# The fold of the input moved into the transform's first products, and the second stage's split and transpose issued two slots ahead

## The chip, the core and the metric

The kernel runs on one core of a Trainium2 chip. The core's engines work side by side, each through a queue of its own in program order: TensorE (PE in the profile, with its weight loads shown as PEld), VectorE (DVE, in the text also V), ScalarE (ACT), GpSimd (POOL) and SyncE (SP), which here issues most of the transfers. The metric is the time in device microseconds (us) that one execution takes.

## The reference

The reference takes eight batches of 3072 x 256 numbers through three steps:

```
X = fft(fft(x, axis=1), axis=2).real                    # 8 x 3072 x 256
x = X.reshape(24576, 256)
h = x @ w_in                                            # 256 -> 2048
x = (max(h, 0) + log1p(exp(-|h|))) @ w_out              # softplus, 2048 -> 256
e = argmax(normalized x . normalized expert_emb / tau)  # one of 8 experts for each token
out = gate * (max(x @ w1[e], 0) @ w2[e])                # 256 -> 1024 -> 256
```

All of it is wanted in 32-bit precision.

## The kernel before

**Numbers in two halves.** TensorE multiplies 16-bit floats, so each operand is split into a high half and a low half, `hi = fp16(v)` and `lo = fp16(v - hi)`, and a product is three matmuls (hi·hi, hi·lo, lo·hi) summed in PSUM.

**First stage: transform, first layer, routing.** It goes through 256 units, each a batch b (8), one of 8 tiles `ti` of 384 tokens and one quarter `i` of the 2048 hidden values. A unit's 64 matmuls are `pu` and `pv` (even and odd part of the first product) and `G` (the product with `w_out`, three units late). ScalarE and VectorE make the softplus of it: `h` (L806, L813, L814), `e` (L822 to L836), and then `gh` and `gl`, the two halves of the scaled result. Per unit either GpSimd makes `gh` in one instruction of 1536 columns (L847) and VectorE makes `gl` for all 1536 (L860), or GpSimd also takes the last 384 columns of both (L847 with 1152, L849, L850, L851) and VectorE's `gl` has 1152. Which of them is decided while the program is written, by a budget for GpSimd in each unit: `room[0]` begins at `ROOM` = 3.6, less 2.6 for each low half of the input that waits for GpSimd and 3.4 for each fold that GpSimd gets, less 1.4 per scatter of routed rows; the longer form of a unit wants 1.2, a step in the preparation of the second stage's weights (`wprep`, L1338 to L1343) wants 2.1 and is held back while `busy[0]` is set.

Beside its 32 units a batch has the next batch's transform done, in two phases. In the first (`fft_a`, `ph[0] == "a"`) a loop over eight pieces `xt` of the input, 96 x 1024 numbers, makes the products `psa` (12 matmuls of 96 columns for each half of a piece, two halves), whose result is evicted into `U_s` by ScalarE (L677) and VectorE (L678). Before a piece can be multiplied it passes three steps, spread over units by the lists `ORDER` and `BORD`: `split_fold` ("sp") replaces its two column halves by their sum and difference (`x_fold`, L490 to L495; for pieces 0, 2, 3, 6 and 7 on VectorE, else on GpSimd), `split_hi` ("sa") scales it (L617) and rounds it to 16 bits (L618) on ScalarE, and `split_lo` ("sq") takes the low half on GpSimd (L610). In the second phase the products `psb`, `psc` and `psd` follow. Batch 0 is transformed ahead of the units, and there the fold is already left to the products: with `boot[0] and PEF`, each `psa` half is 24 matmuls over both column halves of the input, and a negated copy `fan` of the table `fa_s` gives the difference.

**Second stage: the experts.** The routed rows lie sorted by expert in a bucket in DRAM and are taken in 104 slots of up to 256 rows (`phase2`). Slot j: load of the rows of slot j+3 (`p2_load`, SP), `p2_m1(j, 0)` (24 matmuls into `psH`, evicted by ScalarE's `hh` L1209 and VectorE's `hl` L1210), `p2_split(j+1)` (L1179, L1180: two pairs on VectorE that make `xs`), `p2_tr(j+1)` (L1187: SP's DMA transpose of `xs` to `xT`, which `p2_m1(j+1)` multiplies), `p2_m1(j, 1)`, then for slot j+2 the norm (`p2_norm`, L1144 to L1170, on ScalarE, GpSimd and VectorE) with the copy of its expert's weights on VectorE in its middle (L1135), and `p2_m2(j)` (48 matmuls into `psO`, evicted by ScalarE's `ot` L1233, then scattered by GpSimd L1235). `xs` has one buffer, `xT` two, the rows four. `ahead()` is called three times in a slot; from slot 6 to 16 each call issues one of 32 loads of the experts' weights `W` (512 KB each). The generator `phase2` is advanced step by step, three times in each of the last units and once in each turn of the loop that ends the routing.

Instructions are issued on every engine in the order in which the program is written (`tc.manual_schedule`). The line 206 in the profile is the helper that issues every matmul.

Of the kernel before, what the change touches and what calls it, by code (L numbers as in the profile page):

```python
# [11 lines left out]
F16 = mybir.dt.float16  # L12
# [26 lines left out]
ROOM = 3.6  # L39
# [103 lines left out]
def fft_moe_moe(ctx, tc, x, w_in, w128, w_out, emb, tau, w1, w2, fa, db, mcs, tid, ident, tri, misc, out,  # L143
# [27 lines left out]
    fa_s = bigf.tile([96, 2, 96], F16, name="fa_s")  # L171
    xp = pF.enter_context(tc.tile_pool(name="xp", bufs=2, side="right"))
# [178 lines left out]
    fan = bootp.tile([96, 2, 96], F16, name="fan")  # L351
# [250 lines left out]
    def on_v(b, k):  # L602
        return k in (FW1 if b == 1 else FW)

    sp2, sp3 = [], []

    def split_lo():
        for b, k, xt, xh in sp3:
            xl = xp.tile([96, 4, 256], F16, tag="xl", name="xl", bufs=3)
            G.tensor_tensor(xl, xt, xh, op=ALU.subtract)  # L610
            xs[b, k] = (xh, xl)
        sp3.clear()

    def split_hi():
        for b, k, xt in sp2:
            xh = xp.tile([96, 4, 256], F16, tag="xh", name="xh", bufs=3)
            A.activation(xt, xt, AF.Copy, scale=scal[b]["sx"][0:96])  # L617
            A.activation(xh, xt, AF.Copy)  # L618
            sp3.append((b, k, xt, xh))
        sp2.clear()  # L620

    def split_fold():


        for b, k in late:
            xt = xs.pop((b, k))
            x_fold(xt, V if on_v(b, k) else G)
            sp2.append((b, k, xt))
        late.clear()
# [14 lines left out]
    def fft_a(b):  # L644
# [4 lines left out]
        for k in range(8):  # L649
            if k + 2 < 8:  # L650
                x_get(b, k + 2)
            while late and late[0] == (b, k) or sp2 and sp2[0][:2] == (b, k) or sp3 and sp3[0][:2] == (b, k):
                split_lo()
                split_hi()
                split_fold()
            xh, xl = xs.pop((b, k))
            for c in range(2):
                ps = fps("psa")
                for j in range(4):
                    o = ps[:, j * 96:(j + 1) * 96]  # L660
                    cs = slice(c * 128, (c + 1) * 128)
                    if boot[0] and PEF:
# [576 lines left out]
    def phase2():  # L1239
# [5 lines left out]
        p2_split(0)  # L1245
        yield
        p2_tr(0)
        yield
# [6 lines left out]
        for j in range(nslot):  # L1255
# [19 lines left out]
            if j + 1 < nslot:  # L1275
                p2_split(j + 1)
                p2_tr(j + 1)
# [3 lines left out]
            if j + 2 < nslot:  # L1281
# [4 lines left out]
                p2_wcopy(j + 2)  # L1286
                for _ in nrm:
                    pass
# [72 lines left out]
    with tc.manual_schedule():  # L1361
# [89 lines left out]
        for s in range(len(units) + LAG + 1):  # L1451

            room[0] = ROOM - 2.6 * len(sp3) - 3.4 * sum(not on_v(*t) for t in late)
            nsc = min(len(scq), 2 if cur[0] // 8 >= npair - SNAP or len(scq) > 5 else 1) if room[0] > 0 else 0
            room[0] -= 1.4 * nsc
            busy[0] = bool(sp3) or room[0] < 2.1
# [83 lines left out]
            def tail():  # L1540
                if "row1" in p2 and (u is None or not S2[0].get("xs")):
# [8 lines left out]
                       x2=lambda: x2(2), r1=route, r2=route, r3=route, sp=split_fold, sa=split_hi, sq=split_lo, wp=wp.step, sc=lambda: scatters(nsc), p1=tail, p2=tail, p3=tail,  # L1550
# [54 lines left out]
```

## Time and profile before

| what | value |
|---|---|
| median of three runs | 3485.12 us (3482.34 to 3485.62) |
| profiled execution | 3496.98 us |
| its span, first to last instruction | 3495.2 us |
| PE, DVE, ACT, POOL busy | 88%, 80%, 65%, 61% of the span |
| mean granted TensorE clock | 0.957 of full speed |
| softplus sums of the units (L836), first to last start | 122 to 2334 us |
| first-layer matmuls of the experts, first to last start | 2333.4 to 3483.7 us |

The two stages meet at about 2333 us. Busy shares are means over stages with different limits, so a stage is read by its own rows. A wait that the profile lists belongs to the engine that stood, and names the instruction whose end ended it. Rows are given with the line of the kernel, the engine, the operation and the tiles, written as result<-inputs.

### The profile page before, as it was taken

Reading aid. Unit: us, or ns where it says so; the run is one execution under the profiler, and the core shown is the slowest. Engines: PE = TensorE matmul, PEld = TensorE weight load, DVE = VectorE, ACT = ScalarE, POOL = GpSimd, SP = SyncE. Lnnn points to the kernel's source line nnn. Section 1 sums busy time; section 2 is a strip of 40 time slices with the busy share of each in tenths; the row PEclk is TensorE's granted clock in tenths of the full one; section 3 lists DMA queues with packets and bytes.
Section 4 is the critical chain, followed back from the end, with each engine's and each line's share of the span. In section 5 each row is a group of like instructions: output and inputs, shape, how many; then the busy total and the mean of one; then the engine's idle time right before and its main releaser. Section 6 shows DMA issues by size and latency. Waiting matters only on the chain.

```text
span 3495.2 us, 76414 instructions
## 1 busy us (share of the span) xinstructions
PE 3078.9 (88%) x31264; PEld 2740.8 (78%) x31264; DVE 2796.1 (80%) x4488; ACT 2260.5 (65%) x3400; POOL 2138.7 (61%) x1855
## 2 busy tenths in 40 slices
PE   3788898888987988888988999998889999999997
PEld 3677787876876877777887899877778888888886
DVE  7779898988888989988988988984557777777776
ACT  5777777767877878867877888763344444444443
POOL 5357677776786777777777787662234444444443
PEclk8899998998999999999999999999899999999999
DMA  4111210311211211211111000114643333332221
GB/s 138 48 49 53 71 57 28 101 40 38 73 52 51 80 42 62 80 46 51 50 46 31 19 17 20 65 38 107 175 117 76 75 75 80 75 75 74 73 73 38
DMA packets 197088, 223.74 MB, mean 64 GB/s; under 512 B 119028, under 2 KB 154751, under 8 KB 196480
## 3 DMA queue, kind: packets, MB, share of 16 engines
q1 hardware_dynamic: 177920, 167.32, 18.1%
q0 software_dynamic: 18816, 51.54, 4.2%
q8 instruction: 244, 4.00, 0.5%
q14 instruction: 108, 0.88, 0.1%
HBM read 122.91 MB, written 70.71 MB: 55 GB/s over the span
## 4 chain that ended last, share of the span: by engine, by line
issue 29%; PE 24%; DVE 20%; POOL 12%; ACT 10%; DMA 4%; POOLq 0%; SPq 0%; DVEq 0%; ACTq 0%
PE G L206 12%; DVE e L836 5%; PE pu L206 4%; POOL out_dram L1235 3%; DVE gl L860 3%; PE pv L206 3%; ACT e L831 2%; POOL gh L847 2%; ACT e L827 2%; DVE h L814 2%; DVE h L813 2%; PE psb L206 2%; PE psH L206 1%; ACT e L822 1%; POOL xt L495 1%
## 5 line engine op out<-in xcount | busy, mean ns | idle before, releaser
L847 POOL TENSOR_SCALAR gh<-e,sc 128x1536 f16<-128x1536 f32 (+1 forms) x256 | 620.8, 2425 | 493.5 <-DVE e L836 333.2
L206 PE MATMUL G<-wo_s,gh 128*128 128x264 f16 x6144 | 832.7, 284 | 2.2 <-POOL gh L850 2.0
L206 PEld LDWEIGHTS <-gh 128*128 128x128 f16 x6144 | 602.7, 101 | 100.2 <-POOL gh L850 3.3
L206 PE MATMUL psH<-xT,wb 128*128 128x256 f16 (+1 forms) x4992 | 560.3, 274 | 67.1 <-DMA xT<-xs 66.5
L836 DVE SCALAR_TENSOR_TENSOR e<-h,e 128x1536 f32<-128x1536 f32 x256 | 531.6, 2077 | 75.3 <-ACT e L831 71.8
L206 PEld LDWEIGHTS <-wb 128*128 128x128 f16 x4992 | 480.2, 100 | 137.7 <-DMA xT<-xs 78.3
L206 PEld LDWEIGHTS <-win_s 128*128 128x128 f16 x6144 | 534.0, 100 | 24.6 <-DVE h L814 11.6
L206 PE MATMUL psO<-wb,hh 128*128 128x256 f16 x3200 | 529.8, 273 | 0.6 <-ACT hh L1209 0.6
L206 PE MATMUL G<-wo_s,gl 128*128 128x264 f16 x3072 | 440.3, 281 | 28.6 <-DVE gl L860 28.4
L1147 POOL TENSOR_TENSOR nr<-ssq,half 128x2 f32<-128x2 f32 (+1 forms) x104 | 237.5, 2284 | 355.3 <-ACT jk L1144 355.0
L860 DVE SCALAR_TENSOR_TENSOR gl<-e,sc,gh 128x1536 f16<-128x1536 f32 (+1 forms) x256 | 451.0, 1762 | 3.6 <-POOL gh L847 2.2
L206 PE MATMUL psO<-wb,hl 128*128 128x256 f16 x1600 | 436.2, 273 | 0.6 <-DVE hl L1210 0.5
L1209 ACT ACTIVATE hh<-psH 128x512 f16<-128x512 f32 (+1 forms) x416 | 239.6, 579 | 269.7 <-PE psH L206 263.8
L1210 DVE SCALAR_TENSOR_TENSOR hl<-psH,hh 128x512 f16<-128x512 f32 (+1 forms) x416 | 268.7, 666 | 181.4 <-ACT hh L1209 173.3
L822 ACT ACTIVATE e<-h 128x1536 f32<-128x1536 f32 x256 | 378.0, 1477 | 47.7 <-DVE h L814 46.7
L1235 POOL DMA_INDIRECT out_dram<-ot,r x200 | 202.3, 1011 | 311.2 <-ACT ot L1233 272.3
L831 ACT ACTIVATE e<-e 128x1536 f32<-128x1536 f32 x256 | 379.5, 1482 | 4.0
L827 ACT ACTIVATE e<-e 128x1536 f32<-128x1536 f32 x256 | 378.4, 1478 | 0.0
L206 PE MATMUL pu<-pqh,win_s 128*128 128x192 f16 (+1 forms) x2048 | 371.6, 251 | 3.8 <-ACT h L806 3.8
L206 PEld LDWEIGHTS <-gl 128*128 128x128 f16 x3072 | 303.3, 100 | 89.0 <-DVE gl L860 38.5
L206 PEld LDWEIGHTS <-hh 128*128 128x128 f16 x3200 | 312.6, 98 | 36.8 <-ACT hh L1209 0.7
L813 DVE SCALAR_TENSOR_TENSOR h<-pv,sc,h 128x768 f32<-128x768 f32 (+1 forms) x256 | 258.7, 1011 | 99.2 <-ACT h L806 50.5
(274 smaller groups left out, 5902.8 us busy)
## 6 DMA issues: line engine op xcount, KB each, us to landing
xt<-in_x_dram SPq DMA_DIRECT2D x114, 384.0 KB
r<-bucket SPq DMA_DIRECT2D x96, 268.0 KB
wt<-in_w_dram SPq DMA_DIRECT2D x16, 1024.0 KB
wsc<-wo SPq DMA_DIRECT2D x32, 512.0 KB
W<-wsc SPq DMA_DIRECT2D x32, 512.0 KB
raw<-in_w_in_dram SPq DMA_DIRECT2D x8, 512.0 KB
raw<-in_w_out_dram SPq DMA_DIRECT2D x8, 512.0 KB
wb<-wsc SPq DMA_DIRECT2D x2, 2048.0 KB
```

The source lines that it names most:

```text
L206: T.matmul(o, l, r, start=start, stop=stop)
L813: V.scalar_tensor_tensor(h[:, :, n:384], pv[:, :, s0:n], sc["ninv"], h[:, :, s0:n], op0=ALU.mult, op1=ALU.add)
L822: A.activation(e, h, AF.Abs)
L827: A.activation(e, e, AF.Exp, scale=-1.0)
L831: A.activation(e, e, AF.Ln, bias=1.0)
L836: V.scalar_tensor_tensor(flat(d["e"]), flat(d["h"]), 0.0, flat(d["e"]), op0=ALU.max, op1=ALU.add)
L847: G.tensor_scalar(gh[:, 0:n], e[:, 0:n], sg, 1.0, op0=ALU.mult, op1=ALU.mult)
L860: V.scalar_tensor_tensor(flat(d["gl"]), flat(d["e"]), scal[u[0]]["sg"], flat(d["gh"]), op0=ALU.mult, op1=ALU.subtract)
L1147: G.tensor_tensor(nr[:, 0:nt], ssq[:, 0:nt], half[:, 0:nt], op=ALU.pow)
L1209: A.activation(h2, p_, AF.Relu)
L1210: V.scalar_tensor_tensor(l2, p_, 0.0, h2, op0=ALU.max, op1=ALU.subtract)
L1235: no_dep(G.indirect_dma_start(out=out, out_offset=bass.IndirectOffsetOnAxis(ap=rows.bitcast(I32)[:, t, 264:265], axis=0), in_=ot, in_offse ...
```

## The change

In the first stage the fold instructions are gone for batches 1 to 7 too: `psa` is always made of 24 matmuls, with `fan` kept for the whole stage. A piece passes two steps, both straight from the loaded input: ScalarE scales and rounds in one instruction, and the low half is one VectorE instruction (scale and subtract). The "sp" step does nothing. `ROOM` is 4.8 and takes no account of the splits any more, and `busy[0]` is no longer set in the loop.

In the second stage slots 0 and 1 are split and transposed before the loop, and inside slot j it is slot j+2 that is split and transposed: after its weights are copied and the first part of its norm is made, and before `p2_m2(j)`.

```diff
-ROOM = 3.6
+ROOM = 4.8
...
+    fan = bigf.tile([96, 2, 96], F16, name="fan")
...
-    fan = bootp.tile([96, 2, 96], F16, name="fan")
...
+    def split_hi():
+        for b, k in late:
+            xt = xs.pop((b, k))
+            xh = xp.tile([96, 4, 256], F16, tag="xh", name="xh", bufs=3)
+            A.activation(xh, xt, AF.Copy, scale=scal[b]["sx"][0:96])
+            sp3.append((b, k, xt, xh))
+        late.clear()
     def split_lo():
         for b, k, xt, xh in sp3:
             xl = xp.tile([96, 4, 256], F16, tag="xl", name="xl", bufs=3)
-            G.tensor_tensor(xl, xt, xh, op=ALU.subtract)
+            V.scalar_tensor_tensor(xl, xt, scal[b]["sx"][0:96], xh, op0=ALU.mult, op1=ALU.subtract)
...
-    def split_hi():
-        for b, k, xt in sp2:
-            xh = xp.tile([96, 4, 256], F16, tag="xh", name="xh", bufs=3)
-            A.activation(xt, xt, AF.Copy, scale=scal[b]["sx"][0:96])
-            A.activation(xh, xt, AF.Copy)
...
-    def split_fold():
-        for b, k in late:
-            xt = xs.pop((b, k))
-            x_fold(xt, V if on_v(b, k) else G)
...
-                    if boot[0] and PEF:
+                    if PEF:
...
-        p2_split(0)
-        yield
-        p2_tr(0)
-        yield
+        for j in range(min(2, nslot)):
+            p2_split(j)
+            yield
+            p2_tr(j)
+            yield
...
             p2_m1(j, 0)
             yield
             ahead()
-            if j + 1 < nslot:
-                p2_split(j + 1)
-                p2_tr(j + 1)
             p2_m1(j, 1)
...
                 p2_wcopy(j + 2)
+                next(nrm)
+                p2_split(j + 2)
+                p2_tr(j + 2)
                 for _ in nrm:
                     pass
             p2_m2(j)
...
-            room[0] = ROOM - 2.6 * len(sp3) - 3.4 * sum(not on_v(*t) for t in late)
+            room[0] = ROOM
             nsc = min(len(scq), 2 if cur[0] // 8 >= npair - SNAP or len(scq) > 5 else 1) if room[0] > 0 else 0
             room[0] -= 1.4 * nsc
-            busy[0] = bool(sp3) or room[0] < 2.1
```

How the instructions of the engines stand in the program, before and after, at three places.

GpSimd in the first stage, a stretch of batch 3's transform, before (`gh<-e,sc` of 1536 columns is the short form of a unit, `xt<-xt` a fold, `xl` a low half, `bucket` a scatter):

```order
L847 TENSOR_SCALAR gh<-e,sc 128x1536
L490 TENSOR_TENSOR xt<-xt 96x4x128
L494 TENSOR_SCALAR xt<-xt 96x4x128
L495 TENSOR_TENSOR xt<-xt 96x4x128
L847 TENSOR_SCALAR gh<-e,sc 128x1536
L959 MEMSET gap 1x8
L960 DMA bucket<-rows,dst 198912x268
L959 MEMSET gap 1x8
L960 DMA bucket<-rows,dst 198912x268
L610 TENSOR_TENSOR xl<-xt,xh 96x1024
```

The same engine in the same part of the program, after:

```order
L835 TENSOR_SCALAR gh<-e,sc 128x1152
L837 TENSOR_SCALAR e<-e,sc 128x384
L838 TENSOR_SCALAR gh<-e 128x384
L839 TENSOR_TENSOR gl<-e,gh 128x384
L947 MEMSET gap 1x8
L948 DMA bucket<-rows,dst 198912x268
```

Folds and low halves are gone from GpSimd, and the units have the long form: 255 of them in the whole program, before 115. On VectorE 36 folds of two instructions go, 56 instructions `xl<-xt,sc,xh` come, and `gl` has 1152 columns in 255 units.

VectorE in a slot of the second stage, from the evictions of `p2_m1(j, 0)` on, before (`wb<-W` is the weights' copy, `u`, `s`, `nr`, `dn` and `gm` belong to the norm of slot j+2):

```order
L1179 TENSOR_SCALAR xs<-r,s_35404 128x256
L1180 SCALAR_TENSOR_TENSOR xs<-r,s_35404,xs 128x256
L1179 TENSOR_SCALAR xs<-r,s_35404 128x256
L1180 SCALAR_TENSOR_TENSOR xs<-r,s_35404,xs 128x256
L1210 SCALAR_TENSOR_TENSOR hl_35531<-psH,hh_35530 128x512 x2
L1133 TENSOR_LOAD ti__27853
L1133 ISA x2
L1135 ISA
L1135 COPY wb_27850<-W 128x4097
L1150 TENSOR_SCALAR u<-nr 128x2
```

A slot after, from the copy on:

```order
L1123 COPY wb_29387<-W 128x4097
L1138 TENSOR_SCALAR u<-nr 128x2
L1139 TENSOR_SCALAR u<-u 128x2
L1141 TENSOR_SCALAR s_37157<-u 128x2
L1143 TENSOR_SCALAR s_37157<-u 128x2
L1167 TENSOR_SCALAR xs<-r,s_37157 128x256
L1168 SCALAR_TENSOR_TENSOR xs<-r,s_37157,xs 128x256
L1167 TENSOR_SCALAR xs<-r,s_37157 128x256
L1168 SCALAR_TENSOR_TENSOR xs<-r,s_37157,xs 128x256
L1145 TENSOR_SCALAR nr<-nr 128x2
L1146 RECIPROCAL nr<-nr 128x2
L1148 SCALAR_TENSOR_TENSOR u<-r,nr 128x2
```

The four instructions of the split have moved from between the evictions of the slot to behind the weights' copy, ahead of the rest of the norm (`u<-r,nr` is what ScalarE's L1164 waits for).

SP in a slot in which `W` is loaded, before (`r` is the load of rows, `zt` a clearing of rows):

```order
L1113 DMA bucket<-zt 128x268
L1116 DMA W<-wsc 128x2048 x2
L1187 DMA_TRANSPOSE xT<-xs 128x8x128
L1116 DMA W<-wsc 128x2048
L1126 ISA
L1126 DMA r<-bucket 128x2x268
```

And after:

```order
L1101 DMA bucket<-zt 128x268
L1104 DMA W<-wsc 128x2048 x3
L1175 DMA_TRANSPOSE xT<-xs 128x8x128
L1114 ISA
L1114 DMA r<-bucket 128x2x268
```

The transpose stands behind all three weight loads of its slot, and it is that of slot j+2 instead of j+1. The first `W` loads stand in slot 5, before in slot 6.

## Rows read from the trace of the kernel before

**Rows 1.** Busy us by stretch: length, PE, PEld, DVE, ACT, POOL, clock, DMA, GB/s.

```profile
412.00:1988.00 1576.00, 1368.18 (x14743) 1217.75 (x14742) 1389.92 (x1637) 1211.20 (x1337) 1178.84 (x900) 0.95 0.17 52
2104.00:2206.00 102.00, 102.00 (x1037) 93.61 (x1035) 91.42 (x96) 86.72 (x77) 75.87 (x71) 1.00 0.05 18
2600.00:3400.00 800.00, 782.78 (x7130) 695.23 (x7128) 583.26 (x1412) 355.95 (x1039) 357.42 (x370) 1.00 0.31 75
```

**Rows 2.** Lines between 412 and 1988 us: count, duration ns min/median/max.

```profile
L836 DVE SCALAR_TENSOR_TENSOR e<-h,e x178: 1736/1759/4910, 415.2 to 1987.5; 128x1536 f32<-128x1536 f32 x178
...
L860 DVE SCALAR_TENSOR_TENSOR gl<-e,sc,gh x177: 1396/1805/4339, 417.0 to 1982.9; 128x1536 f16<-128x1536 f32 x112, 128x1152 f16<-128x1152 f32 x65
...
L492 DVE SCALAR_TENSOR_TENSOR xt<-xt x29: 686/1487/2495, 499.9 to 1949.4; 96x512 f32<-96x512 f32 x29
...
L847 POOL TENSOR_SCALAR gh<-e,sc x177: 1217/2642/3615, 421.2 to 1983.0; 128x1536 f16<-128x1536 f32 x112, 128x1152 f16<-128x1152 f32 x65
...
L849 POOL TENSOR_SCALAR e<-e,sc x65: 574/579/2301, 480.4 to 1985.4; 128x384 f32<-128x384 f32 x65
...
L851 POOL TENSOR_TENSOR gl<-e,gh x65: 910/916/2295, 481.7 to 1986.6; 128x384 f16<-128x384 f32 x65
...
L610 POOL TENSOR_TENSOR xl<-xt,xh x48: 2121/2140/2892, 411.7 to 1963.0; 96x1024 f16<-96x1024 f32 x48
...
L494 POOL TENSOR_SCALAR xt<-xt x18: 613/2012/2124, 415.3 to 1924.8; 96x512 f32<-96x512 f32 x18
...
L495 POOL TENSOR_TENSOR xt<-xt x18: 1264/2642/2867, 417.5 to 1925.5; 96x512 f32<-96x512 f32 x18
```

**Rows 3.** Timeline, 1098 to 1120 us: start, length, instruction, [idle before <-releaser].

```profile
1098.93 2.14 POOL L610 TENSOR_TENSOR xl<-xt,xh 96x1024 f16<-96x1024 f32 x1
1099.01 4.91 DVE L836 SCALAR_TENSOR_TENSOR e<-h,e 128x1536 f32<-128x1536 f32 x1
...
1107.11 1.54 POOL L847 TENSOR_SCALAR gh<-e,sc 128x1536 f16<-128x1536 f32 x1
1107.15 1.15 ACT L617 ACTIVATE xt<-xt,sc 96x1024 f32<-96x1024 f32 x1 [8.18 <-POOL xt L495]
...
1116.52 1.81 DVE L860 SCALAR_TENSOR_TENSOR gl<-e,sc,gh 128x1536 f16<-128x1536 f32 x1
1116.78 3.49 POOL L847 TENSOR_SCALAR gh<-e,sc 128x1536 f16<-128x1536 f32 x1 [5.12 <-DVE e L836]
```

**Rows 4.** Waits between 412 and 1988 us: total us, times, longest.

```profile
ACT xt L617 <- POOL xt L495: 105.6, 17, 9.1
```

**Rows 5.** PE timeline: first and last of one half's 12 psa matmuls.

```profile
1043.28 0.25 PE L206 MATMUL psa<-fa_s,xh 96*128 96x96 f16 x2
...
1043.75 0.21 PE L206 MATMUL psa<-fa_s,xl 96*128 96x96 f16 x1
```

**Rows 6.** The low half made by VectorE for batch 0.

```profile
L595 DVE SCALAR_TENSOR_TENSOR xl<-xb,sc,xh x4: 1272/1754/3664, 31.6 to 54.4; 96x1024 f16<-96x1024 f32 x4
```

**Rows 7.** Waits of PE for the transposes, whole span.

```profile
PE psH L206 <- DMA xT<-xs: 66.5, 40, 9.7
```

**Rows 8.** The same between 2600 and 3400 us.

```profile
PE psH L206 <- DMA xT<-xs: 17.1, 25, 2.4
```

**Rows 9.** PE timeline: first products of slots 7 and 8.

```profile
2433.29 8.23 PE L206 MATMUL psH<-xT,wb 128*128 128x256 f16 x48 [9.69 <-DMA xT<-xs]
...
2446.59 5.40 PE L206 MATMUL psH<-xT,wb 128*128 128x256 f16 x48
```

**Rows 10.** SP timeline: the issue of slot 7's transpose.

```profile
2425.66 1.94 SPq L1187 DMA_TRANSPOSE xT<-xs  x1
```

**Rows 11.** DVE timeline of one slot: an eviction, first and last of the split.

```profile
2695.20 0.69 DVE L1210 SCALAR_TENSOR_TENSOR hl<-psH,hh 128x512 f16<-128x512 f32 x1 [0.77 <-ACT hh L1209]
...
2697.12 0.34 DVE L1179 TENSOR_SCALAR xs<-r,s 128x256 f16<-128x256 f32 x1
...
2698.28 0.49 DVE L1180 SCALAR_TENSOR_TENSOR xs<-r,s,xs 128x256 f16<-128x256 f32 x1
```

More of the change, by code (lines that the diff above doesn't have):

```diff
@@ L600, in x_split @@
         xs[b, k] = (xh, xl)
-    def on_v(b, k):
-        return k in (FW1 if b == 1 else FW)
-    sp2, sp3 = [], []
+    sp3 = []
+    def split_hi():
[5 more added lines that the diff above has]
+        late.clear()
     def split_lo():
@@ L609, in split_lo @@
             xl = xp.tile([96, 4, 256], F16, tag="xl", name="xl", bufs=3)
-            G.tensor_tensor(xl, xt, xh, op=ALU.subtract)
+            V.scalar_tensor_tensor(xl, xt, scal[b]["sx"][0:96], xh, op0=ALU.mult, op1=ALU.subtract)
             xs[b, k] = (xh, xl)
         sp3.clear()
-    def split_hi():
-        for b, k, xt in sp2:
-            xh = xp.tile([96, 4, 256], F16, tag="xh", name="xh", bufs=3)
-            A.activation(xt, xt, AF.Copy, scale=scal[b]["sx"][0:96])
-            A.activation(xh, xt, AF.Copy)
-            sp3.append((b, k, xt, xh))
-        sp2.clear()
-    def split_fold():
-        for b, k in late:
-            xt = xs.pop((b, k))
-            x_fold(xt, V if on_v(b, k) else G)
-            sp2.append((b, k, xt))
-        late.clear()
     def fft_pre(b):
@@ L651, in fft_a @@
                 x_get(b, k + 2)
-            while late and late[0] == (b, k) or sp2 and sp2[0][:2] == (b, k) or sp3 and sp3[0][:2] == (b, k):
+            while late and late[0] == (b, k) or sp3 and sp3[0][:2] == (b, k):
                 split_lo()
                 split_hi()
-                split_fold()
             xh, xl = xs.pop((b, k))
@@ L1549, in fft_moe_moe @@
                        G0=lambda: g2(0), G1=lambda: g2(1), G2=lambda: g2(2), x0=lambda: x2(0), x1=lambda: x2(1),
-                       x2=lambda: x2(2), r1=route, r2=route, r3=route, sp=split_fold, sa=split_hi, sq=split_lo, wp=wp.step, sc=lambda: scatters(nsc), p1=tail, p2=tail, p3=tail,
+                       x2=lambda: x2(2), r1=route, r2=route, r3=route, sp=lambda: None, sa=split_hi, sq=split_lo, wp=wp.step, sc=lambda: scatters(nsc), p1=tail, p2=tail, p3=tail,
                        wo=boot_w, cb=lambda: cv(0), ck=lambda: cv(1), cp=lambda: cv(2))
```

## The prediction

> **What bounds the kernel now.** I read the busy table by stretches first, since the two stages have different limits. In the long stretch of the first stage, 412 to 1988 us, no engine is full [rows 1]: VectorE is busy 1390 of 1576 us (88%), PE 1368 (87%), ScalarE 1211, GpSimd 1179. The stretch holds 178 units, by the count of the softplus sum `e` [rows 2], so a unit takes 8.85 us. Between 2104 and 2206 us, where batch 7 runs with no transform beside it, PE is busy for all of 102 us; a unit has 64 matmuls, so 1037 make 16.2 units of 6.3 us.
>
> Next the durations by line, because a busy engine may be an engine held up. `e` takes 1.74 us at best and up to 4.91, GpSimd's `gh` 1.22 to 3.62 [rows 2]. The timeline shows why [rows 3]: at 1098.93 GpSimd begins a low half (2.14 us), at 1099.01 VectorE begins `e` and needs 4.91; later `gh` takes 3.49 beside VectorE's `gl`, and 1.54 where VectorE stands. So an instruction of VectorE with two inputs in SBUF and one of GpSimd hardly overlap: one of them stands, and its duration is partly waiting. Shortest durations are therefore the ones to add. For 412 to 1988 us: `e` 178 x 1.74 = 309; `gl` 112 x 1.81 + 65 x 1.40 = 293; VectorE's folds 29 x 2 x 0.69 = 40 (the other instruction taken like L492); `gh` 112 x 1.54 + 65 x 1.22 = 252; the long form's three more 65 x (0.57 + 0.57 + 0.91) = 133 (L850 taken like L849); low halves 48 x 2.12 = 102; GpSimd's folds 18 x (1.26 + 0.61 + 1.26) = 56 (the first taken like L495). That is 1185 us of 1576 [rows 2], before the weights' preparation and the smaller ones, which the change leaves.
>
> Last the waits. ScalarE stands 105.6 us, in 17 waits of up to 9.1 us, for GpSimd's fold [rows 4]; the 8.18 us at 1107.15 [rows 3] is one of them, and nothing of softplus passes ScalarE meanwhile. In the second stage PE is busy 783 of 800 us [rows 1] and waits 17.1 us for the transposes [rows 8]; over the whole stage it is 66.5 us in 40 waits [rows 7], so 49 us lie outside that stretch, most where `W` is loaded.
>
> **First stage, part by part.** *PE:* 56 pieces x 24 = 1344 more matmuls. Twelve of them start from 1043.28 to 1043.75 [rows 5], the last 42 ns before the half is through, so 0.042 us each: 56 us in all, 47 us (48 pieces) in the stretch. PE has 208 us idle there, and this part alone is hidden as long as VectorE and GpSimd are behind PE.
>
> The Trainium skill, in "TensorE: Matmul & The Clock Gate", section "Back-to-back issue gap", says that in a stream of weight loads and matmuls both set the spacing, about 81 ns for 128 columns. By it the 1344 would cost some 109 us, an estimate, and speak against the change. The rows show 42 ns for 96 columns with a weight load each, so I go by the rows.
>
> *VectorE and GpSimd together, shortest durations:* out go both kinds of fold (40 + 56) and the low halves on GpSimd (102). In come 48 low halves on VectorE, 1.27 us at best and 1.75 in the middle [rows 6]: 61 to 84. And `ROOM` gives 112 units of the stretch the long form, where VectorE's `gl` gives back 0.41 and GpSimd takes 1.22 + 0.57 + 0.57 + 0.91 - 1.54 = 1.73 more: 112 x 1.32 = 148. Sum: -198 + 61 + 148 = +11 us. So what the two share does not get less; the work only moves from VectorE to GpSimd and away from the places where one stands in the other's way. VectorE's own time does fall: -40 - 46 + 61 = -25, and what it stood behind low halves and folds.
>
> *ScalarE:* one of two instructions of 1.1 us per piece goes (L617 is 1.15 [rows 3]), hidden, since ScalarE has 365 us idle in the stretch. *The wait of 105.6 us* goes with GpSimd's fold. What is late next is VectorE's new `xl`: it stands first in VectorE's unit, waits for ScalarE's `xh`, and `h`, `e` and `gl` are queued behind it. ScalarE makes `xh` right behind the last softplus instruction of the unit before, while VectorE still has that unit's `e` and `gl` to do (1.74 + 1.40), so I take nothing for it.
>
> Bounds for the stretch: at best all of VectorE's idle time goes, 1576 - 1390 = 186. At worst the shared time fills worse than now (the third rival), +77. Nearest is the row of the wait itself, 105.6; since the long form spends the room that the fold leaves, I take two thirds of it: -70. Ahead of the stretch lie 8 pieces (56 - 48) of like kind: -10. In batch 7, without transforms, some units get 1.3 us more of shared time where nothing was removed, while VectorE and GpSimd are together busy 167 of twice 102 us: +10 (0 to 25). First stage: **-70 us**.
>
> **Second stage.** The transpose is issued behind `p2_m1(j, 1)` for slot j+2, not behind `p2_m1(j, 0)` for slot j+1. Slot 7's was issued at 2425.66 [rows 10] and let PE begin at 2433.29 [rows 9], 7.6 us with weight loads in flight. After the change a whole slot lies between: PE does 783 us for 7130 matmuls [rows 1], 10.5 us for the 96 of a slot. On SP the transpose now has three weight loads ahead of it where two were, some us more, still within 10.5. So I take most waits as gone: 33 of the 49 us, 10 of the 17.1. After a long wait the products themselves are slow, 8.23 us against 5.40 [rows 9]: 2.8 us, five times in the trace, 14 us, of which I take 12. Sum **-55 us** (bounds: -81, all of it; for the other end the fourth rival).
>
> What the split is moved past: from its first to its last instruction it takes 1.65 us (2697.12 to 2698.77) [rows 11], and it now stands ahead of the `u` for which ScalarE's L1164 waits; behind that are queued two `ot` and all `hh` of the next slot, and behind `hh` VectorE's `hl`, which `p2_m2` needs. VectorE has 217 of 800 us idle [rows 1], 0.77 us of a slot just ahead of that `hl` [rows 11]. The split no longer stands between the evictions, so these can follow each other closer, and `p2_m2(j+1)` begins only after 5 us of first products. I take nothing, with 0 to 1.65 us a slot as bounds.
>
> **Sum.** Against the profiled execution of 3497.0 us: 3497 - 70 - 55 = 3372. It lies 11.9 us above the median of the runs, so the forecast for the median is **3360 us**.
>
> **Rivals.** *First, nothing in the first stage.* The shared time of VectorE and GpSimd, not the fold's wait, is the bound: +11 us of work into the same stretch, the 105.6 us are filled with waits of another name. For it: long durations all over [rows 2]. Against it: PE, VectorE and GpSimd are all far from full in the stretch [rows 1]. Time: 3360 + 70 = 3430. The Trainium skill, "SBUF — State Buffer", section "Who interferes with whom", states this: VectorE with two SBUF inputs and a GpSimd instruction that reads SBUF take turns, and the later one stands until the other is through. The rows above agree.
>
> *Second, more.* With no long stalls VectorE and PE fill up: 186 us instead of 70 in the stretch, and 65 in the second stage. For it: 2104 to 2206 us, where PE is full with VectorE at 90%. Against it: GpSimd there has no weights to prepare. Time: 3360 - 116 - 10 = 3234.
>
> *Third, slower: GpSimd's long form in every unit.* Place: units with a weight preparation step, which `busy` no longer holds back. GpSimd's queue is late, `e` and `xl` stand behind its instructions, `gl` behind `gh`, PE behind `gl`. Price: today's stretch is 1576 us; 5% more, as if the turns were taken 5% worse, is 77 us, and with it go the 70. Time: 3360 + 70 + 77 = 3507. It decides from 69 us on, where it eats the second stage's gain as well (1.1 us a unit with one step of preparation). For it: `gh` in the middle takes 2.64 where 1.54 would do [rows 2]. Against it: GpSimd is idle 397 us of the stretch [rows 1].
>
> *Fourth, the split in the second stage's round.* If none of VectorE's idle time can take it, 1.65 us for each of some 98 slots is 162 us, waits for the transposes gone or not: 3360 + 162 = 3522. Against it: those 217 idle us.
>
> *That the change does not do what it says:* `xs` has one buffer, so a split waits for the transpose before it; that one is a whole slot old. I see nothing else.
>
> **Chances.** Forecast 58% (own range 3310 to 3410); first rival 17%, second 12%, third 9%, fourth 4%. The range leaves out the two slower ones and the far half of the second: 3270 to 3475. This kernel's measurement tells 0.2%, 7 us, from no change. Faster: 58 + 17 + 12 = 87, less 1 for the first rival's edge: 86%. Same 3%, slower 11%.
>
> **What would show it.** Right: no wait of ScalarE for a fold; `e` with few durations over 3 us; the stretch of 178 units at about 1500 us; PE's waits for transposes under 25 us and no first products of 8 us. Wrong: GpSimd over 85% busy with `gl` waiting for `gh` (first or third rival); a second-stage slot over 10.8 us with ScalarE's L1164 waiting over 5 us (fourth); PE's psa matmuls spaced by 80 ns.

## The result, and the profile after

The changed kernel takes 3404.47 us (median of four runs, 3397.44 to 3413.82) against 3485.37 us for the one before (four runs, 3482.34 to 3495.64): a ratio of 0.9764, 95% interval 0.9733 to 0.9796. It is faster by 81 us. The forecast was 3360 us, a gain of 125. The gain was two thirds of the one foretold. In the two profiled executions the second stage gave 53.5 of its 55 us and the first 30 of its 70; the runs of each part alone, below, share it out otherwise, 40 and 45.

The profiled execution took 3413.82 us, the longest of the four, with a span of 3411.8. Against the span of before (3495.2) that is 83.4 us less. The first products of the experts began at 2303.5 us instead of 2333.4, so 30 us of it lie ahead of them and 53.5 behind. The rows of before are given by their groups. First the busy table of the same stretches as [rows 1].

```profile
412.00:1988.00 1576.00, 1440.52 (x16399) 1301.79 (x16398) 1320.47 (x1649) 1200.61 (x1331) 1243.44 (x1168) 0.97 0.17 52
2104.00:2206.00 102.00, 99.40 (x1005) 90.25 (x1004) 89.75 (x91) 83.10 (x73) 90.10 (x85) 1.00 0.05 18
2600.00:3400.00 800.00, 790.48 (x7409) 708.23 (x7407) 607.72 (x1470) 339.95 (x1059) 372.38 (x382) 1.00 0.31 75
```

PE has 72 us more to do in the first row and VectorE 69 less; GpSimd went up from 1179 to 1243 us although folds and low halves left it. In batch 7 (second row) PE is no longer full and GpSimd went from 76 to 90 us: there the long form only adds (all 15 units of the row have it, before 10 of 16). In the second stage PE starts 7409 matmuls where it started 7130.

The durations between 412 and 1988 us (count, then ns min/median/max), which answer to [rows 2 and 6]:

```profile
L824 DVE SCALAR_TENSOR_TENSOR e<-h,e x183: 1743/1759/4549, 415.3 to 1982.9; 128x1536 f32<-128x1536 f32 x183
L848 DVE SCALAR_TENSOR_TENSOR gl<-e,sc,gh x183: 1395/1411/2273, 417.1 to 1985.0; 128x1152 f16<-128x1152 f32 x183
L835 POOL TENSOR_SCALAR gh<-e,sc x183: 1214/2317/3434, 417.2 to 1987.2; 128x1152 f16<-128x1152 f32 x183
L839 POOL TENSOR_TENSOR gl<-e,gh x183: 909/916/2367, 412.9 to 1981.0; 128x384 f16<-128x384 f32 x183
...
L616 DVE SCALAR_TENSOR_TENSOR xl<-xt,sc,xh x46: 1270/1282/2842, 500.6 to 1904.0; 96x1024 f16<-96x1024 f32 x46
```

The stretch now holds 183 units where it held 178, 8.61 us each instead of 8.85. That is 5 x 8.61 = 43 us, not 70. All 183 have the long form. But the mean hides two halves. The same count before and after, for 412 to 1340 us and for 1400 to 1988 us (before: L836, after: L824):

```profile
L836 DVE SCALAR_TENSOR_TENSOR e<-h,e x103: 1744/1759/4910, 415.2 to 1339.0; 128x1536 f32<-128x1536 f32 x103
...
L836 DVE SCALAR_TENSOR_TENSOR e<-h,e x69: 1736/1759/4132, 1400.2 to 1987.5; 128x1536 f32<-128x1536 f32 x69
```

```profile
L824 DVE SCALAR_TENSOR_TENSOR e<-h,e x100: 1743/1759/4549, 415.3 to 1337.3; 128x1536 f32<-128x1536 f32 x100
...
L824 DVE SCALAR_TENSOR_TENSOR e<-h,e x77: 1744/1759/2331, 1398.8 to 1982.9; 128x1536 f32<-128x1536 f32 x77
```

Between 412 and 1340 us, where the changed kernel prepares the experts' weights, it does three units *fewer* than before: 9.28 us a unit against 9.01. Behind 1400 us, where the preparation is through (before, it went on), a unit takes 7.64 against 8.52, and PE is busy 576 of 588 us, 98%:

```profile
412.00:1340.00 928.00, 811.47 (x9014) 722.93 (x9013) 762.07 (x989) 659.40 (x739) 733.23 (x670) 0.94 0.19 60
1400.00:1988.00 588.00, 576.20 (x6766) 531.13 (x6763) 504.97 (x608) 497.13 (x548) 458.82 (x457) 0.99 0.12 37
```

The two programs do not do the same between 412 and 1340 us: of the 32 low halves of the experts' weights that the preparation makes (L1332, before L1343) the changed kernel makes 24 there, the one before 20; the last begins at 1370 us, before at 1707. So the gain of the first stage is one large gain and, beside it, a stretch that is no faster (two more profiles of the changed first stage, in runs below, have 101 and 102 units there). The waits between 412 and 1988 us (total us, times, longest) show who is late now:

```profile
ACT xh L609 <- DMA xt<-in_x_dram: 44.7, 5, 14.9
DVE wpm L1302 <- DMA wt<-in_w_dram: 43.9, 12, 5.1
...
PE pv L207 <- DVE wpm L1305: 34.6, 12, 4.7
...
PE G L207 <- POOL gh L838: 21.5, 19, 1.3
```

The 105.6 us that ScalarE stood for folds [rows 4] are gone. In their place ScalarE stands 44.7 us for the input itself, VectorE 43.9 us for the weights `wt` (8.4 us before), PE 34.6 us behind that (27.2 before) and 21.5 us for GpSimd's part of `gh` (2.0 before). All of PE's own waits in the stretch together fell from 206.8 to 134.6 us. What went is mostly its standing for VectorE's evictions and low halves, before and after:

```profile
PE psa L206 <- DVE U_s L678: 52.6, 25, 7.0
...
PE G L206 <- DVE gl L860: 25.4, 28, 3.0
```

```profile
PE psa L207 <- DVE U_s L666: 14.4, 9, 4.4
...
PE G L207 <- DVE gl L848: 3.2, 2, 1.9
```

The timeline of a unit shows GpSimd and VectorE standing for each other as in [rows 3] (start, length, instruction):

```profile
997.53 2.60 DVE L824 SCALAR_TENSOR_TENSOR e<-h,e 128x1536 f32<-128x1536 f32 x1 [0.47 <-ACT e L819]
998.49 2.76 POOL L835 TENSOR_SCALAR gh<-e,sc 128x1152 f16<-128x1152 f32 x1
1001.29 1.74 DVE L848 SCALAR_TENSOR_TENSOR gl<-e,sc,gh 128x1152 f16<-128x1152 f32 x1 [1.04 <-POOL gh L835]
1001.91 1.49 POOL L838 TENSOR_SCALAR gh<-e 128x384 f16<-128x384 f32 x1
...
1005.29 1.22 DVE L1302 TENSOR_REDUCE wpm<-wt 128x1 f32<-128x1024 f32 x1 [2.27 <-DMA wt<-in_w_dram]
```

`gh` of 1152 columns takes 2.76 us beside `e`, where 1.21 would do, VectorE's `gl` waits 1.04 us for it, the 384-column `gh` takes 1.49 beside that `gl` where 0.51 would do, and then VectorE stands 2.27 us for the weights.

In the second stage PE's waits for the transposes, over the whole span [rows 7], are down from 66.5 us to this:

```profile
PE psH L207 <- DMA xT<-xs: 16.4, 8, 3.0
```

Between 2600 and 3400 us none is left [rows 8]. In their place two other waits grew over the whole span, ScalarE's for `u` in the norm and, behind it, PE's for ScalarE's `hh`; before and after:

```profile
ACT lg L1164 <- DVE u L1160: 399.4, 104, 10.9
...
PE psO L206 <- ACT hh L1209: 0.6, 1, 0.6
```

```profile
ACT lg L1152 <- DVE u L1148: 587.9, 104, 11.9
...
PE psO L207 <- ACT hh L1197: 15.3, 7, 6.1
```

While `W` is loaded, the first products of three slots still run slow, 7.04 to 7.08 us, where [rows 9] had 8.23; slots 7, 8 and 9:

```profile
2393.00 5.40 PE L207 MATMUL psH<-xT,wb 128*128 128x256 f16 x48
2405.41 5.41 PE L207 MATMUL psH<-xT,wb 128*128 128x256 f16 x48 [1.77 <-DMA xT<-xs]
2419.14 7.08 PE L207 MATMUL psH<-xT,wb 128*128 128x256 f16 x48 [2.73 <-DMA xT<-xs]
```

### The profile page after: what moved, and what is told of

The parts are those of the page before. It is cut to its first block, busy times and chain, and to the rows that moved or that the text cites. A ratio compares the mean times of both kernels' runs of the same rounds, so it can differ in the third digit from the quotient of the medians.

```text
span 3411.8 us, 79327 instructions
## 1 busy us (share of the span) xinstructions
PE 3101.5 (91%) x32608; PEld 2785.5 (82%) x32608; DVE 2704.9 (79%) x4472; ACT 2180.3 (64%) x3344; POOL 2221.3 (65%) x2159
## 4 chain that ended last, share of the span: by engine, by line
issue 27%; PE 26%; POOL 22%; DVE 13%; ACT 6%; DMA 6%; SPq 0%; POOLq 0%; DVEq 0%; ACTq 0%
PE G L207 13%; PE pu L207 4%; POOL out_dram L1223 4%; POOL bucket L948 3%; PE pv L207 3%; DVE e L824 3%; POOL gh L835 3%; POOL gl L839 2%; DMA xt<-in_x_dram 2%; PE psa L207 2%; POOL gh L838 2%; POOL wo L1332 2%; ACT e L819 2%; POOL e L837 2%; DMA wt<-in_w_dram 2%
## 5 line engine op out<-in xcount | busy, mean ns | idle before, releaser
L835 POOL TENSOR_SCALAR gh<-e,sc 128x1152 f16<-128x1152 f32 (+1 forms) x256 | 494.2, 1930 | 403.0 <-DVE e L824 348.9
L207 PEld LDWEIGHTS <-gh 128*128 128x128 f16 x6144 | 595.2, 100 | 139.7 <-POOL gh L838 39.8
L824 DVE SCALAR_TENSOR_TENSOR e<-h,e 128x1536 f32<-128x1536 f32 x256 | 500.1, 1953 | 100.3 <-ACT e L819 97.9
L207 PE MATMUL psH<-xT,wb 128*128 128x256 f16 (+1 forms) x4992 | 547.0, 270 | 16.5 <-DMA xT<-xs 16.4
L207 PE MATMUL psO<-wb,hh 128*128 128x256 f16 x3200 | 531.9, 273 | 15.3 <-ACT hh L1197 15.3
L1152 ACT ACTIVATE lg<-r,u,nr 128x8 f32<-128x8 f32 x200 | 77.0, 385 | 587.9 <-DVE u L1148 587.9
L848 DVE SCALAR_TENSOR_TENSOR gl<-e,sc,gh 128x1152 f16<-128x1152 f32 (+1 forms) x256 | 393.9, 1539 | 23.1 <-POOL gh L835 23.1
L1198 DVE SCALAR_TENSOR_TENSOR hl<-psH,hh 128x512 f16<-128x512 f32 (+1 forms) x416 | 259.8, 665 | 81.7 <-ACT hh L1197 74.3
```

The lines of the kernel that those rows point to most:

```text
L207: T.matmul(o, l, r, start=start, stop=stop)
L824: V.scalar_tensor_tensor(flat(d["e"]), flat(d["h"]), 0.0, flat(d["e"]), op0=ALU.max, op1=ALU.add)
L835: G.tensor_scalar(gh[:, 0:n], e[:, 0:n], sg, 1.0, op0=ALU.mult, op1=ALU.mult)
L848: V.scalar_tensor_tensor(flat(d["gl"]), flat(d["e"]), scal[u[0]]["sg"], flat(d["gh"]), op0=ALU.mult, op1=ALU.subtract)
L1198: V.scalar_tensor_tensor(l2, p_, 0.0, h2, op0=ALU.max, op1=ALU.subtract)
```

## The experiments

Two theories of the first stage's missing gain stood against each other. **A:** in the units with a preparation step, VectorE's instructions with two SBUF inputs and GpSimd's take turns, and the long form, now in every unit, spent what the fold had freed. **B:** VectorE's own time is the bound, and the long form helps. Later came **C:** GpSimd's own queue is full there, whatever its instructions touch. Medians are of four runs (five for the last kernel); each ratio is against runs of the kernel before on the same chip.

### The two stages apart

The kernel before with only the second-stage part of the diff:

```diff
...
-            if j + 1 < nslot:
-                p2_split(j + 1)
-                p2_tr(j + 1)
...
+                next(nrm)
+                p2_split(j + 2)
+                p2_tr(j + 2)
```

> The kernel before with the second stage's part of the change alone (split and transpose two slots ahead). If the parts are independent, as the two traces suggest (from the first first-layer matmul to the end 1161.8 us before, 1108.2 us after), it takes 53 us less than before: 3432 us (3422 to 3442). If the parts help each other, because GpSimd's free time at the end of the first stage matters to the second, it takes only 30 less or even fewer: over 3450.

Measured: 3444.36 us, ratio 0.989 (0.9862 to 0.9919), 40 us less than the 3484.13 before. Then the changed kernel with these lines, and the ones ahead of the loop, as before:

> The changed kernel with the second stage as before, so only the first stage's part (fold in the products, ROOM 4.8, no low halves on GpSimd). Independent parts: 3485 - 30 = 3455 us (3445 to 3465), and the first-layer matmuls of the experts begin at about 2303 us. If the first stage's part had brought the 70 us of my forecast and the second stage had taken some of it away: 3415 to 3430.

Measured: 3438.66 us, ratio 0.9867 (0.9843 to 0.989), 45.5 us less. The first products, and PE's waits for the transposes, of the second stage's part alone and of the first stage's part alone:

```profile
L206 PE MATMUL psH<-xT,wb x4992: 218/273/422, 2331.8 to 3431.4; 128*128 128x256 f16 x185, 128*128 128x128 f16 x15
...
PE psH L206 <- DMA xT<-xs: 17.6, 8, 4.8
```

```profile
L207 PE MATMUL psH<-xT,wb x4992: 219/273/421, 2286.2 to 3428.1; 128*128 128x256 f16 x185, 128*128 128x128 f16 x15
...
PE psH L207 <- DMA xT<-xs: 59.7, 38, 8.2
```

The parts add up (40 + 45.5 = 85.5, both together 81). From the first to the last of these products it is 1099.6 us in the one and 1141.9 in the other (1150.3 in the kernel before). PE's waits for `hh` are 13.0 us in the one and 0.7 in the other, so it is the second stage's part that brings them. Each median lies outside its expected window, by 2 and by 6 us, in opposite directions. The first stage's part is worth 45 us in medians, more than the 30 of the one profiled execution, whose run was the longest of four: in the second profile the experts' first products begin 47 us earlier than in the kernel before. Likewise the 53.5 of the second stage are in part the doing of the profiled execution of before, 12 us above its median; with the second stage as before, the second profile here, it is 1153.5 us from the first of these products to the end, and 1111.1 with the second stage's part alone. Neither part gave its 70 or 55.

### The long form

The changed kernel where no unit has the long form:

```diff
-GP, GPC, GLB = (0, 1, 2, 3), 1.2, 2
+GP, GPC, GLB = (), 1.2, 2
```

> The changed kernel where GpSimd never takes the long form: it makes gh in one instruction, VectorE makes gl for all 1536 columns. Theory A: in the units with a weight preparation step VectorE's two-input instructions and GpSimd's instructions take turns, and the long form adds 1.3 us a unit to what they share. Without it these 124 units lose 0.5 to 1.2 us each: 60 to 150 us less than after, 3255 to 3345 us. Theory B: VectorE's own time is the bound, and the long form helps by the 0.41 us of gl that it takes off VectorE: 256 x 0.41 = 105 us more, in part hidden, 3440 to 3510 us. A third possibility, that both balance: 3404 within 10 us, with fewer us in the units with preparation and more in those without.

Measured: 3330.28 us, ratio 0.9551 (0.9523 to 0.9578): 74 us less than the changed kernel. Theory B, which asked for 3440 us or more, is out. In 412 to 1340 us it does 108 units, 8 more; in 1400 to 1988, where PE is the bound anyway, 76, one fewer:

```profile
L824 DVE SCALAR_TENSOR_TENSOR e<-h,e x108: 1744/1759/4127, 412.2 to 1335.7; 128x1536 f32<-128x1536 f32 x108
...
L824 DVE SCALAR_TENSOR_TENSOR e<-h,e x76: 1741/1758/2004, 1405.7 to 1982.4; 128x1536 f32<-128x1536 f32 x76
```

Then with a higher price, which takes the long form from the units with a scatter and a preparation step together:

```diff
-GP, GPC, GLB = (0, 1, 2, 3), 1.2, 2
+GP, GPC, GLB = (0, 1, 2, 3), 1.4, 2
```

> The changed kernel with the price of the long form raised from 1.2 to 1.4 in GpSimd's budget: a unit that has both a preparation step (2.1) and a scatter (1.4) of the budget of 4.8 then takes the short form, 61 of the 256 units, the others keep the long form. Theory A: these 61 units, the fullest, lose 0.5 to 1.2 us each: 3330 to 3375 us, between the changed kernel and the one that never takes the long form. Theory B: 0 to 25 us more than the changed kernel, 3404 to 3430 us.

Measured: 3325.86 us, ratio 0.9548 (0.9522 to 0.9573). A had it between the two, and it does not lie there: taking the long form from these units (61 have the short form now, one had it already) brings as much as taking it from all. The loss sat in the units with three loads on GpSimd. The price that the prediction worked out for the long form, 1.32 us a unit, fits there: 60 x 1.32 = 79, and 79 us were measured (75 by the two ratios). For the 195 others it would make 257 us, but the run with none of them is not faster, it is 4 us slower. So the sum of the shortest durations is the price of the turns in the fullest units and not in the others.

### Turns or GpSimd's own time

To the kernel that never takes the long form, GpSimd work of like length was added behind every `gh`, once of a kind that reads nothing and once of a kind that reads SBUF (the results are used nowhere):

```diff
...
+            for _ in range(4):
+                G.memset(gdum[0], 0.0)
```

> The kernel that never takes the long form (3330 us), with four clearings of a tile of 128 x 384 added on GpSimd behind every gh: about the time of the long form's additional instructions (1.7 us a unit), but they read nothing in SBUF. Theory A (instructions of VectorE and GpSimd that read SBUF take turns, and the long form adds to that): the clearings cost nothing to speak of, 3320 to 3345 us. Theory C (GpSimd's own queue is full in the units with preparation, whatever its instructions touch): most of the 74 us come back, 3380 to 3415 us.

Measured: 3364.11 us, ratio 0.9655 (0.9631 to 0.9678), 34 us more than without the clearings: between the theories. Then scalings instead of the clearings (and one clearing ahead of the units):

```diff
...
-            for _ in range(4):
-                G.memset(gdum[0], 0.0)
+            for _ in range(3):
+                G.tensor_scalar(gdum[0], gdum[0], 1.0, 1.0, op0=ALU.mult, op1=ALU.mult)
```

> As the kernel with clearings in place of the long form, but the four clearings (417 ns each) are three scalings of the same 128 x 384 tile in place (about 0.5 us each), so GpSimd has as much time added and now reads SBUF. Theory A for the other half of the 74 us (taking turns): about 35 us more than with clearings, 3390 to 3420 us. Theory C alone (only GpSimd's own time counts): the same as with clearings or, with 0.1 us a unit less, a little under: 3350 to 3368 us.

Measured: 3459.26 us, ratio 0.9919 (0.9897 to 0.9942), 95 us more than with the clearings (92 by the ratios), well past what A asked for. The two added instructions over the whole program, clearings first (ns min/median/max):

```profile
L845 POOL MEMSET gdum<- x1024: 407/417/447, 128.9 to 2257.2; 128x384 f16 x171
```

```profile
L846 POOL TENSOR_SCALAR gdum<-gdum x768: 502/512/2112, 122.7 to 2349.8; 128x384 f16<-128x384 f16 x192
```

Undisturbed, the clearings come to 1024 x 0.417 = 427 us and the scalings to 768 x 0.512 = 393, so GpSimd has less to do in the second. But no clearing ever took over 0.447 us, while a scaling took up to 2.11. In the timeline with clearings VectorE's `e` keeps its 1.76 us beside them:

```profile
1008.20 1.84 POOL L845 MEMSET gdum<- 128x384 f16 x4
1008.81 1.76 DVE L824 SCALAR_TENSOR_TENSOR e<-h,e 128x1536 f32<-128x1536 f32 x1 [0.36 <-ACT e L819]
```

Both theories hold a part: GpSimd's added time alone costs 34 us (C), and that an addition reads SBUF costs 95 more (A). How the 74 us of the long form divide between the two these runs do not tell: the scalings take nothing off VectorE, the long form takes 0.41 us of `gl` a unit. The Trainium skill, in "SBUF — State Buffer", section "Who interferes with whom", makes the same distinction, an instruction that only writes being free of VectorE's second input; the 0.417 and the 2.11 us agree.

### The fold without the larger budget

The changed kernel with the old budget (131 long forms):

```diff
-ROOM = 4.8
+ROOM = 3.6
...
-            room[0] = ROOM
+            room[0] = ROOM - 2.6 * len(sp3) - 3.4 * sum(t[1] not in (FW1 if t[0] == 1 else FW) for t in late)
...
+            busy[0] = bool(sp3) or room[0] < 2.1
```

> The changed kernel with the GpSimd budget as before: 3.6 less what the splits would cost, and the preparation held back as before; 131 long forms instead of 255. So the fold and the low halves leave and nothing is given back to GpSimd. Theory A: the larger budget cost 60 to 100 us, and without it the kernel takes 3310 to 3345 us. If the long form is harmful only together with a scatter and a step of preparation in one unit, which the smaller budget excludes: at the lower end, 3315 us. If the fold itself gave only the 45 us and the budget nothing: 3404 us.

Measured: 3306.7 us, ratio 0.9497 (0.9476 to 0.9518), below the expected window. Against the second stage's part alone (3444.36) the fold and the low halves are worth 138 us, and the larger budget gives back 98 (3404.47 - 3306.7; 93 by the ratios). The 98 are not the long form's alone: with the old budget the preparation is also held back, and its last step begins at 1556 us instead of 1370.

### VectorE's wait for the weights

The load of `wt` stands one unit earlier against the maximum `wpm` that reads it:

```diff
             yield
             yield
+            yield
             m = sm.tile([128, 2], F32, tag="wpm", name="wpm")
...
                 SY.dma_start(dst[:, :, cs], wo)
-                yield
+                if c == 0:
+                    yield
```

> The changed kernel with the load of each half of the experts' weights issued one unit earlier against VectorE's maximum that reads it; the preparation has as many steps per half as before. The profile of the changed kernel has VectorE waiting 46.9 us in 13 waits for this load (8.4 us in 4 before), and PE behind it. Theory E: this wait is a cause of its own, and without it 30 to 50 us go: 3355 to 3375 us. Theory A/C: GpSimd is behind in these units, the load is late only because the buffer comes free late, and another wait for GpSimd takes its place: 3390 to 3410 us.

Measured: 3404.2 us, ratio 0.9756 (0.9738 to 0.9775): nothing. VectorE's wait is still there, over the whole span 41.2 us where the changed kernel had 46.9:

```profile
DVE wpm L1303 <- DMA wt<-in_w_dram: 41.2, 14, 5.5
```

The trace of this run shows why. The load stands on SP behind the store of GpSimd's last `wo` of the half before, here GpSimd's instruction, then SP's store and load:

```profile
990.83 2.13 POOL L1333 TENSOR_TENSOR wo<-wt,wo 128x1024 f16<-128x1024 f32 x1
```

```profile
992.99 0.41 SPq L1334 DMA_DIRECT2D wsc<-wo  x1
993.44 0.46 SPq L1295 DMA_DIRECT2D wt<-in_w_dram  x1
```

The maximum begins at 999.59, 6.2 us behind that load. In the changed kernel the load is issued at 998.99, also right behind the store, and the maximum begins at 1005.29, 6.3 us later. All 12 of these loads between 412 and 1340 us stand so in both traces: GpSimd sets when they start, and the edit did not take the wait away. What the wait is worth by itself was therefore not tested; theory E is neither shown nor excluded.

### Spreading the preparation

The preparation steps only in units without a scatter, once with the long form where none of them meets it (`GPC` = 1.4), once never with it:

```diff
-                while busy[0] or not pool_room(2.1):
+                while busy[0] or not pool_room(3.5):
...
```

> The kernel with long form only where no preparation meets it, and the preparation steps only in units without a scatter (price 3.5 instead of 2.1), so that they spread over about 190 units instead of 124. Theory A: the turns per unit fall by about 0.6 us in the units that were fullest, and the later units have PE as bound anyway: 3275 to 3310 us. If each step of preparation costs the same wherever it stands: 3325 us as without the spreading. Theory D, the units' time is set by late hand-offs and not by the sum of the turns: 3326 to 3350.

> As the spread preparation, and the long form never taken. Theory A: the turns in units with a scatter are fewer, 3.35 instead of 4.67 us for gh and gl, but VectorE has 0.4 us more in each: 3265 to 3310 us, within 15 us of the kernel with spread preparation and the long form. If VectorE's time is now the bound: 20 to 40 us more than that one.

Measured: 3296.43 us, ratio 0.9467 (0.9445 to 0.9489), and 3290.9 us, ratio 0.945 (0.9429 to 0.947). In 412 to 1340 us both do 116 units, 8.0 us each; the row of the second:

```profile
L824 DVE SCALAR_TENSOR_TENSOR e<-h,e x116: 1735/1758/3331, 413.8 to 1334.4; 128x1536 f32<-128x1536 f32 x116
```

Without the spreading, the same two kernels took 3325.86 and 3330.28 us. So of GpSimd's steps it counts how many stand in one unit. (Part of the 116 units is work put off: the preparation now goes on until 2040 us.) Going back to the lower price from unit 160 on, so that batch 7 is free of them, did not pay:

```diff
-                while busy[0] or not pool_room(3.5):
+                while busy[0] or not pool_room(3.5 if cur[0] < 160 else 2.1):
...
```

> The fastest so far (long form never taken, preparation only in units without a scatter), where from unit 160 on a scatter no longer keeps the preparation out, so that it is through before the last batch, whose units took 7.0 us with it and 6.4 without. Gain of up to 10 us if the units before don't get longer by as much: 3278 to 3292 us, against 3291.

Measured: 3298.16 us, ratio 0.9452 (0.9434 to 0.947), against 0.945 (0.9429 to 0.947) without that edit: the two can't be told apart by these ratios, and the gain hoped for did not come.

### The third weight load behind the transpose

The kernel with spread preparation and without the long form, and with the third weight load of a slot moved:

```diff
             p2_m1(j, 1)
             yield
-            ahead()
...
                 p2_tr(j + 2)
                 for _ in nrm:
                     pass
+            ahead()
             p2_m2(j)
```

> The fastest so far (3291 us), with the third weight load of a second-stage slot issued behind the transpose of that slot instead of ahead of it. If the transposes are late in slots 5 to 16 because of SP's order, as the four waits of 0.7 to 2.7 us in the changed kernel suggest: 8 to 18 us less, 3273 to 3283 us, and slots 5 to 20 take 170 to 178 us instead of 186. If the transfers themselves are what the slots wait for, whatever their order: 3291 within 5 us, and slots 5 to 20 stay over 182 us.

Measured: 3283.64 us (3278.14 to 3288.6), ratio 0.9409 (0.9393 to 0.9424). PE's waits for the transposes in this kernel:

```profile
PE psH L207 <- DMA xT<-xs: 9.6, 6, 3.2
```

They were 16.5 us in 8 waits without the edit, and slots 5 to 20 take 181.8 us instead of 186.0 by the starts of their first products. By medians the edit gave 7 us, by the ratios to the kernel before some 14. The slots fit neither expectation (170 to 178, or over 182). What holds the rest of them is not shown: PE still waits 14.1 us for `hh` (15.2 without the edit), and VectorE's split now stands 17.0 us for the transpose before it (8.6). This is the fastest of all: 121 us below the changed kernel, 3491 - 3284 = 207 below the one before.

## Why the prediction was half right

**PE's 1344 more matmuls** were sized right. In the changed kernel the psa matmuls start 0.13 us after three others, 43 ns each, against the 42 ns of [rows 5], and where nothing else is late PE is the bound at 7.64 us a unit, so there these matmuls are not hidden (an estimate from the 43 ns: 8 pieces of 24 on 32 units are 0.26 us a unit):

```profile
1046.07 0.25 PE L207 MATMUL psa<-fa_s,xh 96*128 96x96 f16 x2
1046.16 0.20 PE L207 MATMUL psa<-fa_s,xl 96*128 96x96 f16 x1
1046.20 0.25 PE L207 MATMUL psa<-fa_s,xh 96*128 96x96 f16 x2
```

**The sum of turns**, +11 us for the stretch, was wrong as a sum: the part gained 45. Its terms fared differently. Fold and low halves were to take 137 away (160 for all 56 pieces at the same prices); the runs measured 138 for the whole program. The long form was to give 148 back for 112 units; taking it from every unit brought 74 us, and taking it from the 60 units alone that have a preparation step and a scatter as well brought 79. In the others it cost nothing that was measured.

**The step of the first stage that failed** is the one behind that sum: "Nearest is the row of the wait itself, 105.6; since the long form spends the room that the fold leaves, I take two thirds of it: -70". A wait of ScalarE, an engine with 365 us idle, was taken as the price, and a third of it as the cost of the larger budget. Measured are 138 us for fold and low halves and 98 back for the larger budget: both were taken too small, and in the difference, 40 to 45 instead of 70, much of the two errors cancels, which is luck. The stretch gave 43 us (183 units for 178). What the end of ScalarE's wait is worth by itself no run here tells.

**The third rival**, GpSimd's long form in the units with preparation, was real, with its place as named (units with a preparation step, PE waiting for `gh`), and with nearly its price: 77 us were named, 74 to 98 measured. It did not decide because it was set against a fold that brings nothing, and the fold brought more than the long form took. (The prediction has it decide from 69 us on; by its own terms, with 55 for the second stage, that would be from 55 on.) The gain behind 1400 us, 0.88 us a unit, I did not foresee. The earlier end of the preparation does not explain it: the kernel with the preparation spread and no long form makes 11 of the 32 low halves of the weights there (the one before made 8) and has 76 units in that stretch, against 77 in the changed kernel and 69 before. What these kernels share against the one before is that fold and low halves are gone from GpSimd. The bare claim that "what the two share does not get less" left out that the place of a step in the program counts.

**Batch 7** was given +10 us. PE started 1005 matmuls in 102 us instead of 1037: 3% of 16 to 17 units of 6.4 us, some 3 us in that half of the batch, within the 0 to 25 named.

**The second stage** was given -55 and gave -53.5 in the two profiled executions, -40 in the medians of the run with that part alone. Waits for the transposes fell by 50.1 (43 were taken); of the slow first products three of 7.1 us are left where six of 7.1 to 8.3 stood, some 10 us gained where I took 12. **The step that failed** is "I take nothing" for the split's new place ahead of `u`: ScalarE's wait for `u` grew from 3.8 to 5.7 us a slot, about the 1.65 us that the split takes, and behind it PE's waits for `hh` grew from 0.6 to 15.3 us. With these 15 us the sum would have been -40. So the fourth rival was real with a tenth of its 162 us. The longest of these waits, 6.1 us, stands in slot 5, where VectorE itself was late, so not all of them need be the split's. The rows of one slot after, VectorE's first and last of the split, then `hl`, and ScalarE's wait for `u`, which answer to [rows 11]:

```profile
2698.98 0.35 DVE L1167 TENSOR_SCALAR xs<-r,s 128x256 f16<-128x256 f32 x1
...
2700.16 0.48 DVE L1168 SCALAR_TENSOR_TENSOR xs<-r,s,xs 128x256 f16<-128x256 f32 x1
...
2701.16 0.39 ACT L1152 ACTIVATE lg<-r,u,nr 128x8 f32<-128x8 f32 x1 [5.57 <-DVE u L1148]
...
2703.25 1.29 DVE L1198 SCALAR_TENSOR_TENSOR hl<-psH,hh 128x512 f16<-128x512 f32 x2 [0.57 <-ACT hh L1197]
```

ScalarE waits 5.57 us here for `u` (3.93 in a slot before), over the 5 us that I had named as one half of the rival's sign. The other half, a slot over 10.8 us, is not seen here: `hl` waits 0.57 us where it waited 0.77, and from one slot's first products to the next it is 10.49 us (2510.44 to 2520.93), the 10.5 of 96 matmuls that the forecast had. The cost sits in the few slots where PE stands for `hh`, 7 waits in the whole stage.

## What to carry to other kernels

When two engines take turns, add up the shortest durations of all that takes part, unit by unit and not over a stage: here the sum was the price in the fullest units (79 us by sum and by measurement) and counted for nothing in the others. A long wait of a third engine with idle time to spare shows that something is late, not what it costs. An engine's idle time does not make a move free either: the split fitted into VectorE's 217 idle us, and still PE stood 15 us for what was queued behind it. What a change frees on an engine is not to be spent again by the same change without counting the unit that is fullest already: here the long form in 60 of 256 units, those with three loads on GpSimd, cost 79 us. Look at halves of a stage, not its mean, when a step of the program ends at another time than before, and check with a run that moves that end before calling it the cause.

## What the runs showed of the hardware

A clearing on GpSimd that reads nothing runs at its own pace beside VectorE's two-input instructions (407 to 447 ns in 1024 of them), a scaling of the same tile in place took 502 to 2112 ns. Between the kernels with the one and with the other lie 95 us of 3400.

In the stretch where the units were slowest, the granted clock of PE was lowest, a mean over its two levels of 1.2 and 2.4 GHz: 0.94 of the higher in 412 to 1340 us of the changed kernel with PE busy 811 of 928 us, 0.97 in the same stretch of the kernel without the long form with PE busy 850 us (and 0.95 at 9.01 us a unit in the kernel before, 0.99 at 8.0 with the preparation spread and no long form):

```profile
412.00:1340.00 928.00, 850.16 (x9742) 766.32 (x9740) 859.32 (x1038) 709.32 (x787) 625.15 (x396) 0.97 0.20 65
```

Whether the lower clock added to the time, and how much of the 74 us it is, was not tried.
